# A fused attention and MoE kernel: one query load on another queue, seven more dummy matmuls near the start

## The chip, the cores and the metric

The kernel runs on one core of a Trainium2 chip. A core has five engines with their own instruction streams: TensorE (matrix products), VectorE, ScalarE, GpSimd (elementwise work) and SyncE (which here only issues transfers). ScalarE issues transfers too, on a queue of its own. The metric is device time in microseconds, the median over several runs.

## The reference

```python
q_s = exp(q - max(q, -1));  q_s /= sum(q_s, -1)      # softmax over the head's 64 columns
k_s = exp(k - max(k, 2));   k_s /= sum(k_s, 2)       # softmax over the 576 tokens
kv  = einsum('bhsd,bhse->bhde', k_s, v)              # 64 x 64 per batch and head
att = einsum('bhsd,bhde->bhse', q_s, kv)
x   = att.transpose(0, 2, 1, 3).reshape(4608, 512)
h   = x @ w_in                                       # 512 -> 2048
out = (h * sigmoid(beta * h)) @ w_out                # 2048 -> 512
```

There are 8 batches, 8 heads, 576 tokens and 64 columns per head, all float32.

## The kernel before, in words

**Slabs.** The 4608 tokens are cut into nine slabs: slab t (0 to 7) has the first 512 tokens of batch t, slab 8 the 64 that are left of each batch. For each slab there is a first pass (x times w_in, 16 groups f of 128 hidden columns, four matmuls m each, then SiLU on ScalarE into GT) and a second pass (GT times w_out into the output). Beside them, on ticks counted by matmuls, run the attention pieces of the next batches.

**Attention.** Heads go in pairs hp (0 to 3), 128 rows of the array together. For a pair: exp of Q and K on ScalarE (`exp_q`, `exp_kc`), cast of V (`cast_v`), normalisation of Q (`norm_main`: a reduction and a reciprocal on VectorE, a multiplication on VectorE or GpSimd), a turn of Q by four matmuls against the identity (`t_steps`) and a copy, the key-value product (18 small matmuls, `kv_tiles` or `kv_prods`), its scaling, and the output product with the turned Q (`out_now` or `out_prods`), whose result is copied into XT, the input of the first pass. From batch 2 on the turn is made by a DMA.

**The start.** Batch 0 has nothing to hide behind, so its pieces are written out by hand (lines 598 to 634). `warm(3, 0, True)` puts three long fp32 matmuls on zeros in front; `warm(n, bk)` puts n short bf16 ones (128x512, on the zeros of WARM) into bank bk. None of their results is used. Batch 0's order on TensorE is: long dummies, turn of pair 0, turns of beta (`turn_beta`), turn of pair 1, key-value product of pair 0, then by turns dummies, turns, key-value and output products of the later pairs, then the first matmuls of the first pass.

**Queues.** The order of loads is the order of `add` calls for each issuing engine. Line 291 loads batch 0's Q: pairs 0 and 2 whole on SyncE's queue, the four heads of pairs 1 and 3 (2, 3, 6, 7) one by one on ScalarE's, then beta (BT) there. SyncE goes on with K and V of batch 0 pair by pair, then w_in in twelve pieces, then w_out and batch 1. Every operation names what it reads and writes; `plan` turns this into waits on counters, and each engine works its own list in order.

**Batch 1** is worked during the second pass of slab 0 by the list `todo`: turns at ticks 104 and 109, key-value products in two halves at ticks 115 and 127. Its V pairs 1 to 3 are cast by GpSimd.

Of the kernel before, what the change touches and what calls it, by code (L numbers as in the profile page):

```python
# [29 lines left out]
PE, ACTE, DVE, POOL, SP = "tensor", "scalar", "vector", "gpsimd", "sync"  # L30
# [13 lines left out]
class Program:  # L44
# [12 lines left out]
    def add(self, eng, fn, r=(), w=(), bank=(), slot=None, after=()):  # L57
        op = Op(eng, fn, slot)
        op.pos = len(self.ops)
        deps = op.deps  # L60
        deps.extend(after)
        for k in r:
            deps.extend(self.writer.get(k, ()))
            self.readers.setdefault(k, []).append(op)
        for k in w:
            for d in self.readers.get(k, ()):
                if d is not op and not self._same(d, op):
                    deps.append(d)
            for d in self.writer.get(k, ()):
                if not self._same(d, op):  # L70
                    deps.append(d)
            self.readers[k] = []
            self.writer[k] = [op]
        for k in bank:
            t = self.touch.setdefault(k, {})
            for e, d in t.items():
                if e != eng:
                    deps.append(d)
            t[eng] = op
        if eng == POOL and slot is None:  # L80
            if self.pool is not None:
                deps.append(self.pool)
            self.pool = op
        self.ops.append(op)
        return op
# [78 lines left out]
def bass_efficient_attn_shen__then__act_swish_beta_kernel(  # L164
# [9 lines left out]
    qt_h, kt_h, vt_h = q.tensor, k.tensor, v.tensor  # L174
    win_h, wout_h, beta_h, out_h = moe_w_in.tensor, moe_w_out.tensor, moe_beta.tensor, out.tensor

    with ExitStack() as es:
        def sb(name, shape, dt):
            return es.enter_context(nc.sbuf_tensor(name, shape, dt))
# [4 lines left out]
        QF = [sb(f"QF{i}", [128, H, 4, D], F32) for i in range(2)]  # L184
# [38 lines left out]
        add = P.add  # L223
# [14 lines left out]
        def src(th, b, h0, nh):  # L238
            return bass.AP(th, (b * H + h0) * S * D, [[4 * D, 128], [S * D, nh], [1, 4 * D]])

        def dst(t, h0, nh):
            return bass.AP(t, h0 * 4 * D, [[H * 4 * D, 128], [4 * D, nh], [1, 4 * D]])
# [46 lines left out]


        for hp in range(NHP):
            eng = ACTE if hp % 2 else SP
            if hp % 2 == 0:
                add(eng, lambda e, hp=hp: e.dma_start(dst(QF[0], 2 * hp, 2), src(qt_h, 0, 2 * hp, 2)),
                    w=[("qf", 0, hp, hp // 2)], slot=f"qf0{hp}")
                continue
            for c in range(2):
                h = 2 * hp + c
                add(eng, lambda e, hp=hp, c=c, h=h: e.dma_start(  # L299
                    dst(QF[0], 2 * hp + 1 - c, 1), src(qt_h, 0, h, 1)),  # L300
                    w=[("qf", 0, hp, 2 + c)], slot=f"qf0{h}")
        add(ACTE, lambda e: e.dma_start(BT[:, :], bass.AP(beta_h, 0, [[512, 4], [1, 512]])),
# [29 lines left out]
        def norm_main(b, hp0, n, eng=DVE):  # L332
            i = b % 2
            a = bass.AP(EQ[i], hp0 * 512, [[2048, 128], [64, 8 * n], [1, 64]])
            s_ = bass.AP(QS[i], hp0 * 8, [[32, 128], [1, 8 * n]])
            v_ = bass.AP(QI[i], hp0 * 8, [[32, 128], [1, 8 * n]])
            vb = bass.AP(QI[i], hp0 * 8, [[32, 128], [1, 8 * n], [0, 64]])
            ks = [("eq", i, hp) for hp in range(hp0, hp0 + n)]
            add(DVE, lambda e: e.tensor_reduce(s_, a, AX.X, ALU.add), r=ks, w=[("qs", i, hp0)])  # L339
            add(DVE, lambda e: e.reciprocal(v_, s_), r=[("qs", i, hp0)], w=[("qi", i, hp0)])  # L340
            add(eng, lambda e: e.tensor_tensor(a, a, vb, ALU.mult), r=ks + [("qi", i, hp0)],  # L341
                w=ks)
# [22 lines left out]
        def bank(pool=MB):  # L365
            rot[0] += 1
            return pool[rot[0] % len(pool)]

        def mm(o, l, r_, start, stop, r=(), w=(), bk=0, tr=False, tp=None):
            if tr:  # L370
                add(PE, lambda e: e.transpose(o, l, r_), r=r, w=w, bank=[bk])  # L371
            else:
                add(PE, lambda e: e.matmul(o, l, r_, start=start, stop=stop, tile_position=tp),  # L373
                    r=r, w=w, bank=[bk])

        def t_steps(b, hps, pool=MB, eng=DVE):
            i = b % 2
            st = {}

            def one(n, hp, j):  # L380
                if n == 0 and j == 0:
                    st["b"] = bank(pool)
                p = PS[st["b"]]
                pb = p[:, :].bitcast(BF16)
                c = n * 512 + j * 128
                mm(pb[:, c:c + 128], bass.AP(EQ[i], hp * 512 + j * 128, [[2048, 128], [1, 128]]),
                   IDB[:, :], True, True, r=[("eq", i, hp), "idb"], w=[("ps", st["b"])],
                   bk=st["b"], tr=True)
                if n == len(hps) - 1 and j == 3:
                    w = len(hps) * 512  # L390
                    o = bass.AP(QT[i], hps[0] * 512, [[2048, 128], [1, w]])
                    add(eng, lambda e: (e.copy if eng == ACTE else e.tensor_copy)(o, pb[:, 0:w]),
                        r=[("ps", st["b"])], w=[("qt", i, h) for h in hps], bank=[st["b"]])
            return [lambda n=n, hp=hp, j=j: one(n, hp, j) for n, hp in enumerate(hps)
                    for j in range(4)]
# [110 lines left out]
        def warm(n, bk, long=False):  # L506
            for _ in range(n):
                if long:
                    mm(PS[bk][:, :], bass.AP(XT8, 0, [[NM * SM, 128], [1, 256]]).bitcast(F32),
                       bass.AP(XT8, 0, [[NM * SM, 128], [1, 1024]]).bitcast(F32), True, True,  # L510
                       r=["xw"], w=[("ps", bk)], bk=bk)
                else:
                    mm(PS[bk][:, :], WARM[:, 0:128], WARM[:, :], True, True, r=["warm"],
                       w=[("ps", bk)], bk=bk)
# [17 lines left out]
        def out_now(b, hp, bk, eng):  # L532
            i = b % 2
            for c in (0, 64):
                p = slice(c, c + 64)
                tile_mm(bk, c, 64 - c if hp % 2 else c, 0, SM, KVC[2][p, hp, :], QT[0][p, hp, :], True, True,
                        [("kvc", 2, hp), ("qt", 0, hp)])
            add(eng, lambda e: (e.copy if eng == ACTE else e.tensor_copy)(
                XT[i][:, hp, :], PS[bk][:, :]),
                r=[("ps", bk)], w=[("xt", i, hp)], bank=[bk])  # L540

        def go(steps):
            for s in steps:
                s()
# [28 lines left out]
        def cast_win(c, m, eng):  # L573
            add(eng, lambda e: e.tensor_copy(WIN[:, m, 512 * c:512 * c + 512], STAGE[c][:, m, :]),
                r=[SKEY[c][m]], w=[("win", c, m)])
# [3 lines left out]
        def turn_beta():  # L579
            for g, n, o in ((4, 4, 0), (2, 2, 0), (2, 2, 256)):  # L580
                for k_ in range(n):
                    mm(bass.AP(PS[KB], 16 + o // 128 + k_, [[512, 128], [4, g]]),
                       bass.AP(BT, o + k_, [[512, g], [n, 128]]), IDF[0:g, 0:g],
                       True, True, r=["bt", "idf"], w=[("ps", KB)], bk=KB, tr=True)
# [23 lines left out]
                cast_v(0, hp, ACTE)  # L608
        norm_main(0, 0, 1)
        norm_main(0, 1, 1, POOL)  # L610
        go(t_steps(0, (0,), (3,)))
        turn_beta()
        norm_main(0, 2, 1, POOL)
        norm_main(0, 3, 1, POOL)
# [14 lines left out]
        kv_tiles(2, 7)  # L629
        out_now(0, 1, 5, ACTE)  # L630
        cast_win(0, 0, DVE)
        warm(1, 3)
        out_now(0, 2, 0, ACTE)
        kv_tiles(3, 1)

# [1 line left out]

        def pass1_mm(t, f, m, bk):
            x = XT8 if t == 8 else XT[t % 2]
            rd = [("xt8", 0)] + [("xt8", p_, y) for p_ in range(1, 4) for y in range(2)] if t == 8 else [("xt", t % 2, m)]  # L640
            n = 2 if f < 8 else 4
            l = bass.AP(WIN, m * DFF + 128 * (f // n * n) + f % n, [[NM * DFF, 128], [n, 128]])
            mm(PS[bk][:, :], l, x[:, m, :], m == 0, m == NM - 1,
               r=rd + [("win", f // 4, m)], w=[("ps", bk)], bk=bk)
            if m == NM - 1:
                add(ACTE, lambda e: e.activation(GT[:, f, :], PS[bk][:, :], ACT.Silu,  # L646
                                                 scale=BETA[:, f:f + 1]),
                    r=[("ps", bk), "beta"], w=[("gt", f)], bank=[bk])
# [244 lines left out]
```

## Time and profile before

| what | value |
|---|---|
| median of 4 runs | 281.03 us (280.86 to 281.48) |
| profiled execution: time, span | 281.66 us, 279.8 us |
| TensorE busy | 270.8 us, 97% of the span |
| ScalarE, VectorE, GpSimd busy | 166.4, 102.9, 33.1 us |
| mean granted TensorE clock | 0.988 |
| HBM read, written | 36.71 MB, 9.44 MB |
| first matmul, first matmul of the first pass | 1.45 us, 16.03 us |

The span is from the first to the last instruction; the time has in addition what lies around it, 1.86 us in this execution. Matmul records carry modelled ends, so a busy TensorE may still run at half its clock; the granted clock is a column of its own. In a timeline row stand the start, the busy time, the engine, the line, what is written from what, and in brackets the idle time before it with its releaser. All matmuls are issued on line 373, all turns on line 371, so they are told apart by tiles.

### The profile page before, as it was taken

How to read it: one execution, taken by the hardware profiler on the slowest of the kernel's cores; microseconds unless marked ns; L12 is line 12 of the kernel's file. 1: busy time of each engine (PE TensorE's matmuls, PEld its weight loads, DVE VectorE, ACT ScalarE, POOL GpSimd, SP SyncE). 2: the span in 40 equal slices, each digit the busy share in tenths (PEclk: the TensorE clock that was granted, in tenths of full speed). 3: DMA queues.
4: the chain of work that ended last, by engine and by line, in shares of the span. 5: the costliest groups of instructions: out<-in, count | busy, mean ns of one | idle time of the engine just before them, and what ended most of it. 6: DMA issues, size and time to landing. Idle time of an engine off the chain costs nothing.

```text
span 279.8 us, 4581 instructions
## 1 busy us (share of the span) xinstructions
PE 270.8 (97%) x1892; PEld 131.8 (47%) x1922; DVE 102.9 (37%) x206; ACT 166.4 (59%) x240; POOL 33.1 (12%) x50
## 2 busy tenths in 40 slices
PE   6899999999999999999999999999999999999995
PEld 2545454454445454545454544444444444444443
DVE  3664595007590158305640463035603300110012
ACT  4657867789767835794479537853751276017500
POOL 2630041306100305030002100000000000000000
PEclk9689999999999999999999999999999999999999
DMA  7999999996279999960499134001600120011022
GB/s 224 389 387 402 388 389 374 375 380 113 41 238 389 200 356 290 374 147 2 144 357 234 39 130 95 2 4 75 169 0 2 47 103 2 0 73 77 2 71 79
DMA packets 42173, 50.12 MB, mean 179 GB/s; under 512 B 21028, under 2 KB 29476, under 8 KB 41000
## 3 DMA queue, kind: packets, MB, share of 16 engines
q1 hardware_dynamic: 41168, 48.77, 53.9%
q10 hardware_dynamic: 984, 1.06, 1.2%
q8 instruction: 15, 0.25, 0.4%
q14 instruction: 6, 0.05, 0.1%
HBM read 36.71 MB, written 9.44 MB: 165 GB/s over the span
## 4 chain that ended last, share of the span: by engine, by line
PE 94%; DMA 2%; issue 1%; ACTq 0%; ACT 0%; DVE 0%
PE PS L373 93%; DMA QF<-in_q_dram 2%; PE PS L371 1%; ACTq L299 0%; ACT EK L323 0%; ACT VB L358 0%; DVE O2S L722 0%; ACT EQ L315 0%; ACTq L147 0%
## 5 line engine op out<-in xcount | busy, mean ns | idle before, releaser
L646 ACT ACTIVATE GT<-PS,BETA 128x512 bf16<-128x512 f32 x144 | 96.7, 689 | 61.4 <-PE PS L373 61.4
L373 PE MATMUL PS<-WOUT,GT 128*128 128x512 bf16 (+2 forms) x573 | 125.0, 373 | 1.8 <-issue 1.3
L373 PE MATMUL PS<-XT,WIN 128*128 128x512 bf16 x566 | 125.7, 379 | 0.7 <-issue 0.2
L373 PEld LDWEIGHTS PS<-XT,WIN 128*128 128x128 bf16 x576 | 60.4, 106 | 63.6 <-ACT GT L646 0.4
L373 PEld LDWEIGHTS PS<-WOUT,GT 128*128 128x128 bf16 x592 | 56.5, 98 | 65.9 <-issue 1.1
L701 DVE COPY O2S<-PS 128x512 f32<-128x512 f32 x33 | 22.7, 688 | 124.3 <-PE PS L373 124.3
L358 POOL CAST VB<-VF 128x576 bf16<-128x576 f32 x29 | 20.8, 716 | 85.2 <-DMA VF<-in_v_dram 83.8
L339 DVE TENSOR_REDUCE QS<-EQ 128x8 f32<-128x512 bf16 (+1 forms) x22 | 20.1, 912 | 20.1 <-ACT EQ L315 20.0
L460 ACT CAST XT<-PS 128x512 bf16<-128x512 f32 x14 | 7.6, 588 | 23.9 <-PE PS L373 23.9
L323 ACT ACTIVATE EK<-KF 128x1152 bf16<-128x1152 f32 (+1 forms) x19 | 18.4, 1004 | 1.7 <-DMA KF<-in_k_dram 1.7
L315 ACT ACTIVATE EQ<-QF 128x512 bf16<-128x512 f32 x32 | 17.6, 615 | 3.0 <-DMA QF<-in_q_dram 3.0
L341 DVE TENSOR_TENSOR EQ<-EQ,QI 128x1024 bf16<-128x1024 bf16 (+1 forms) x14 | 16.2, 1158 | 0.5
L460 DVE CAST XT<-PS 128x512 bf16<-128x512 f32 x14 | 9.1, 686 | 13.4 <-PE PS L373 13.4
L341 POOL TENSOR_TENSOR EQ<-EQ,QI 128x512 bf16<-128x512 bf16 x8 | 8.3, 1042 | 34.9 <-DVE QI L340 34.5
L373 PEld LDWEIGHTS PS<-VB,EK 64*64 64x64 bf16 x576 | 7.3, 112 | 5.2 <-issue 2.5
L373 PE MATMUL PS<-VB,EK 64*64 64x65 bf16 x576 | 8.7, 199 | 0.9 <-ACT VB L358 0.5
L373 PE MATMUL PS<-QT,KVC 64*64 64x512 bf16 x64 | 6.8, 404 | 0.0
L646 ACT ACT_TABLE_LOAD x5 | 6.4, 1283 | 0.1
L373 PE MATMUL PS<-XT 128*128 128x512 f32 x6 | 4.9, 982 | 1.4 <-DVE XT L226 1.4
L340 DVE RECIPROCAL QI<-QS 128x8 f32<-128x8 f32 (+1 forms) x22 | 5.0, 226 | 0.8
L323 ACT ACT_TABLE_LOAD x4 | 5.1, 1283 | 0.1
L444 DVE TENSOR_TENSOR KVC<-PS,RC 128x128 bf16<-128x128 f32 (+1 forms) x16 | 4.4, 274 | 0.6
(51 smaller groups left out, 66.9 us busy)
## 6 DMA issues: line engine op xcount, KB each, us to landing
out_dram<-O2S SPq DMA_DIRECT2D x8, 1024.0 KB, 4.3
QF<-in_q_dram SPq DMA_DIRECT2D x30, 256.0 KB, 5.7
KF<-in_k_dram SPq DMA_DIRECT2D x6, 1152.0 KB, 8.1
VF<-in_v_dram SPq DMA_DIRECT2D x6, 1152.0 KB, 11.3
KF<-in_k_dram SPq DMA_DIRECT2D x8, 288.0 KB, 8.5
VF<-in_v_dram SPq DMA_DIRECT2D x8, 288.0 KB, 9.1
WST<-in_moe_w_in_dram SPq DMA_DIRECT2D x8, 256.0 KB, 7.6
O2S<-in_moe_w_in_dram SPq DMA_DIRECT2D x4, 512.0 KB, 11.0
```

The costliest lines, as they stand in the source:

```text
L315: add(ACTE, lambda e, o=o, a=a: e.activation(o, a, ACT.Exp), r=[("qf", i, hp, x) for x in ((2, 3) if hp % 2 else (hp // 2,))], w=[("eq", i ...
L323: add(ACTE, lambda e: e.activation(o, a, ACT.Exp), r=[("kf", i, h) for h in range(hp, hp + n)], w=[("ekc", i, h) for h in range(hp, hp + n)])
L339: add(DVE, lambda e: e.tensor_reduce(s_, a, AX.X, ALU.add), r=ks, w=[("qs", i, hp0)])
L340: add(DVE, lambda e: e.reciprocal(v_, s_), r=[("qs", i, hp0)], w=[("qi", i, hp0)])
L341: add(eng, lambda e: e.tensor_tensor(a, a, vb, ALU.mult), r=ks + [("qi", i, hp0)], w=ks)
L358: add(eng, lambda e: (e.copy if eng == ACTE else e.tensor_copy)(o, a), r=[("vf", i, hp), ("vone", i)], w=[("vb", i, hp, h) for h in ((0, 1 ...
L371: add(PE, lambda e: e.transpose(o, l, r_), r=r, w=w, bank=[bk])
L373: add(PE, lambda e: e.matmul(o, l, r_, start=start, stop=stop, tile_position=tp), r=r, w=w, bank=[bk])
L444: add(DVE, lambda e, o=o, p_=p_, vb=vb: e.tensor_tensor(o, p_, vb, ALU.mult), r=[("ps", bk)] + [("rc", i, hp) for hp in hps], w=[("kvc", k ...
L460: add(eng, lambda e, eng=eng, bk=bk, hp=hp: (e.copy if eng == ACTE else e.tensor_copy)(XT[i][:, hp, :], PS[bk][:, :]), r=[("ps", bk)], w=[ ...
L646: add(ACTE, lambda e: e.activation(GT[:, f, :], PS[bk][:, :], ACT.Silu, scale=BETA[:, f:f + 1]), r=[("ps", bk), "beta"], w=[("gt", f)], ba ...
L701: add(eng, lambda e: (e.copy if eng == ACTE else e.tensor_copy)(O2S[t % 2][:, u, :], PS[bk][:, :]), r=[("ps", bk)], w=[("o2", t % 2, u)], ...
```

## The change

Four edits. In the load loop, head 7 is issued by SyncE and no longer by ScalarE. Three short dummies are put in front of the turn of pair 0 and three behind it, in front of beta's turns. In front of the output product of pair 2 (the third) stand two short dummies in place of one. The list of what slab 8's first pass reads now names both halves of each of the four remainder pieces, where it named for the first piece a key that nothing writes.

```diff
         for hp in range(NHP):
-            eng = ACTE if hp % 2 else SP
             if hp % 2 == 0:
-                add(eng, lambda e, hp=hp: e.dma_start(dst(QF[0], 2 * hp, 2), src(qt_h, 0, 2 * hp, 2)),
+                add(SP, lambda e, hp=hp: e.dma_start(dst(QF[0], 2 * hp, 2), src(qt_h, 0, 2 * hp, 2)),
                     w=[("qf", 0, hp, hp // 2)], slot=f"qf0{hp}")
                 continue
             for c in range(2):
                 h = 2 * hp + c
-                add(eng, lambda e, hp=hp, c=c, h=h: e.dma_start(
+                add(SP if h == 7 else ACTE, lambda e, hp=hp, c=c, h=h: e.dma_start(
                     dst(QF[0], 2 * hp + 1 - c, 1), src(qt_h, 0, h, 1)),
                     w=[("qf", 0, hp, 2 + c)], slot=f"qf0{h}")
...
         norm_main(0, 1, 1, POOL)
+        warm(3, 0)
         go(t_steps(0, (0,), (3,)))
+        warm(3, 0)
         turn_beta()
...
         cast_win(0, 0, DVE)
-        warm(1, 3)
+        warm(2, 3)
         out_now(0, 2, 0, ACTE)
         kv_tiles(3, 1)
...
-            rd = [("xt8", 0)] + [("xt8", p_, y) for p_ in range(1, 4) for y in range(2)] if t == 8 else [("xt", t % 2, m)]
+            rd = ([("xt8", p_, y) for p_ in range(4) for y in range(2)] if t == 8
+                  else [("xt", t % 2, m)])
```

## The prediction

> **What bounds it now.** I began with the page: the chain of waits names TensorE for nearly everything, and the slices show its clock dipping only in the second and third slice (6 and 8 tenths). So the time is set by when TensorE gets into its dense stretch and by what interrupts it. Next I cut the start into stretches of 3.41 us, moving their edges until the granted clock was constant inside each:
>
> ```profile
> PE 94%; DMA 2%; issue 1%; ACTq 0%; ACT 0%; DVE 0%
> ```
> ```profile
> core 0: us, PE busy (x), PEclk, DMA share, GB/s
> 5.63:9.04 3.41, 2.21 (x14) 1.00 0.98 357
> 9.04:12.45 3.41, 2.85 (x36) 0.50 1.02 388
> 12.45:15.86 3.41, 3.05 (x61) 0.50 1.05 393
> 15.86:19.27 3.41, 3.36 (x28) 1.00 1.07 396
> ```
>
> The third figure from the right is the clock: full until 9.04, half until 15.86, then full to the end. Two equal steps of 3.41 us say that a monitor looks at fixed windows. The chain in order of time then shows what TensorE sat on before 10.20, and the timeline the waits:
>
> ```profile
> 2.17 6.14 DMA QF<-in_q_dram
> ...
> 8.39 0.07 ACT EQ L315
> 8.46 0.47 issue
> 8.92 0.67 ACT EK L323
> 9.59 0.57 ACT VB L358
> 10.16 0.04 issue
> 10.20 1.25 PE PS L373 x19
> ```
> ```profile
> 7.87 1.11 PE L371 MATMUL PS<-IDF,BT 4*128 4x4 f32 x8 [0.38 <-DMA BT<-in_moe_beta_dram]
> ...
> 8.39 0.63 ACT L315 ACTIVATE EQ<-QF 128x512 bf16<-128x512 f32 x1 [2.07 <-DMA QF<-in_q_dram]
> ...
> 11.51 0.66 POOL L358 CAST VB<-VF 128x576 bf16<-128x576 f32 x1 [0.28 <-DMA VF<-in_v_dram]
> ...
> 12.99 0.67 POOL L358 CAST VB<-VF 128x576 bf16<-128x576 f32 x1 [0.81 <-DMA VF<-in_v_dram]
> ...
> 14.34 2.85 POOL L574 CAST WIN<-WST 128x512 bf16<-128x512 f32 x4 [0.68 <-DMA WST<-in_moe_w_in_dram]
> ...
> 44.31 0.67 POOL L358 CAST VB<-VF 128x576 bf16<-128x576 f32 x1 [0.86 <-DMA VF<-in_v_dram]
> ...
> 45.84 0.48 PE L373 MATMUL PS<-VB,EK 64*64 64x65 bf16 x36
> ```
>
> In brackets stands the idle time and what ended it. Two things hold the start: ScalarE stands 2.07 us for head 7 (issued at 2.17, landed 8.31), and TensorE crawls at half clock from 9.04 to 15.86 with no gap left in it. The last two rows matter for the end: batch 1's fourth head pair is cast at 44.98 (44.31 + 0.67) and used at 45.84.
>
> **The queue.** Head 7 leaves ScalarE's queue (four issues of 0.47) for SyncE's, third there. Landings before, as issue plus time to landing: SyncE's heads 0,1 at 3.9 and heads 4,5 at 5.1; ScalarE's head 6 at 7.2, head 7 at 8.3; K pair 0 at 7.6, V pair 0 at 8.5, K and V pair 1 at 9.2 and 9.9, K pair 2 10.7. [...] Head 7 stands behind 5.1 with 128 KB against an equal partner: both it and head 6 land at about 6.0 (between 5.5 and, if head 6 doesn't profit, 7.2), so exp of pair 3 starts at 6.4 behind its predecessor (ends 6.32) and not at 8.39.
>
> What it is moved ahead of: twelve K, V loads and then all weight loads on SyncE's queue, issued 0.47 us later. The DMA share is 1.0 in nearly every microsecond from 6 to 50 and K, V land 6 to 7 us after issue, so they wait for bytes, not for the issue. By K pair 0 there are 83 KB more ahead of it: 0.23 us later, 7.8. From V pair 0 on the bytes ahead are the same: no shift (bounds: 0.3 earlier, since the dip at 5 to 6 us with share 0.71 could fill; 0.47 later, if the issue counted). Beta's load, now behind three heads and not four, lands before 7.87.
>
> ScalarE then: exp Q3 to 6.95, wait, exp K0 7.85 to 8.5, cast V0 to 9.15, exp K1 9.25 to 9.9, cast V1 to 10.6, exp K2 to 11.4, exp K3 12.2 to 12.9 (lands 12.21). The first key-value product may start at 9.2 instead of 10.20, **1.0 us**.
>
> **The dummies.** A 512-column bf16 matmul streams 0.216 us at full clock (steady spacing in the trace: 0.2157), 0.43 at half. Three start as the fp32 ones end (four passes at 0.85 each issue, last stream ends 5.9) and are through by 6.6, the first turn is ready at 7.1 (VectorE's normalisation): covered. Three more run 7.35 to 8.0; beta's turns follow, 1.1 us, to 9.1, against 8.98 now; the second turn waits for GpSimd until 9.05. Cost 0.1, and it dies in the wait to 9.2. The seventh costs 0.216 at full clock ahead of the third output product, where TensorE waits for V pair 3 until 13.7: nothing. Without this cover: 0.43 at half clock.
>
> What they buy is the clock. Columns streamed in 5.63:9.04 before: fp32 tail 0.27 us, four turns 0.21: about 14% of the window. With six dummies (1.28 us): 51%. The next windows at full clock hold 54 to 71% and 86%. At half clock, 9.04:12.45 held 68 to 86% (the products pair up or not) and was not enough to reopen; the next, full, was. So closing lies somewhere above 14%; no row shows 51%. [...] Gain if the gate stays open: half of the streaming; loss if it doesn't: bounded below. I take open, since 51% is a true filling and no longer an idle window.
>
> **The start, summed** at full clock: first product 9.2 to 9.6; second turn ready at 10.1 (GpSimd 9.03 + 1.04); second product after cast V1, 10.65; third turn after GpSimd's third pass, 11.25; third product after GpSimd's cast of V2, 12.2; output, two dummies, output to 13.45; fourth product after cast V3 (13.66) 13.7 to 14.05; first weight tile landed 13.6, cast by VectorE about 14.1; its four matmuls to 15.0; last output product; second row of weights at **15.25 against 17.33: 2.1 us**. GpSimd's casts of row 1, 2, 3 end at 15.05, 15.76, 16.5, needed 15.25, 16.1, 17.0: they fit.
>
> **What is late next.** From 17.33 TensorE is continuous. Moved by 2.1 us it meets loads whose landing is set by bytes: the last w_in cast ends 25.12 and is needed at 26.1, fits. Batch 1's first turn, now 38.93: w_out rows 8 to 11 land at 33.6 (VectorE scales them 35.09 now), then reduce 0.7, reciprocal 0.2, GpSimd 1.08, so 37.4: gain left 1.5. Second turn, two more reductions and a multiply behind: 39.05 against 40.43, left 1.4. Then the two rows shown last: V pair 3 of batch 1 lands at 44.2 and no byte before it is saved, so its product can't start before 45.05. It starts now at 45.84. **Left: 0.79 us.** After it, nothing in the list of TensorE's waits depends on a load; the later stages shift as one.
>
> The sum is against the profiled execution: 279.8 span, 281.66 with what lies around it, so 279.0 and 280.87. The median of the runs is 281.03, 0.63 lower; I move it by the same 0.79: **280.2 us**. The changed wait list of the last slab adds no instruction: slab 8's first product reads data that VectorE wrote long before.
>
> **Rivals.** *Gate falls at 9.04 all the same* and reopens at 15.86: the dense half-clock run starts at 9.66 (second turn ends) and not 10.20, and has one more dummy of 0.43: 0.11 gained, 280.9. For it: the unknown threshold. Against: a run packed from 9.05 may reopen at 12.45, which gives the forecast again.
>
> *Slower: the gate falls one window later*, at 12.45, because 9.04:12.45 with its waits for V1, GpSimd and V2 holds as little as 54%, and stays shut until 19.27. Then by 19.27 the dense part has run 0.32 + 1.7 us of full-speed work, where now it has 3.0: 1.0 lost, no load covers it, **282.0**. It decides if closing lies above 54 to 71%. Against: at half clock the work from 12.45 is packed, which reopened the gate at 15.86 before; then 0.68 is gained.
>
> *More*: the dip at 5 to 6 us fills or the queue change otherwise advances V by 0.3 to 0.6: the gain is then 1.1 to 1.4, 279.8.
>
> *The DMA shift is real*, 0.47 later everywhere: 0.79 - 0.47 = 0.3, 280.7; I count it to the forecast's lower part.
>
> **Numbers.** Forecast 0.55 (0.04 of it too small to see), gate falls early 0.22, slower 0.15, more 0.08. What can be told from no change is 0.2%, 0.56 us. Faster 0.51 + 0.08 = 0.59; slower 0.15 + 0.03 of the early fall with a dummy in the way; the rest, 0.23, within. Range 279.8 to 281.3: the clipped gain with its bounds, the early fall, and part of the slower case.
>
> **What would show it.** Clock 1.00 in 9.04:12.45 and 12.45:15.86; exp of Q pair 3 before 7; weights' second row near 15.3; the second turn's GpSimd release unmoved at 9.05; a wait of TensorE for GpSimd's VB cast at about 45. If that wait is missing with a gain under 0.8, the start fell short; if the clock is 0.50 after 12.45 in dense matmuls, I am wrong in sign.

## The result, and the profile after

| | before | changed |
|---|---|---|
| median | 281.11 us (63 runs) | 280.55 us (44 runs) |
| ratio, 95% interval | | 0.9982 (0.9975 to 0.9990) |
| profiled execution: time, span | 281.66, 279.8 us | 281.19, 279.4 us |
| second row of slab 0's weights starts | 17.34 us | 15.34 us |

The changed kernel is faster by 0.56 us, or 0.2%; 280.2 us was forecast, 0.91 us below the median of the kernel before in this table. The ratio came back in two later comparisons of the same pair: 0.9982 (0.9972 to 0.9992) and 0.9975 (0.9965 to 0.9986).

The granted clock of the changed kernel, by stretches of 3.41 us, follows; the third figure from the right is the clock. "Gate" is a name for whatever halves it: closed is a clock of 0.50 in that column, open one of 1.00. In the kept trace of this execution the first clock record, of 1.00, starts at 4.92 us (the last section has the weight loads on both sides of it), so the stretches are laid from about there.

```profile
core 0: us, PE busy (x), PEclk, DMA share, GB/s
4.97:8.38 3.41, 3.41 (x20) 1.00 0.98 335
8.38:11.79 3.41, 2.81 (x55) 1.00 1.05 399
11.79:15.20 3.41, 2.81 (x47) 1.00 1.02 379
```

In this execution the gate no longer closes: 1.00 in all three stretches. Next is the page's chain of work that ended last, which was TensorE for 94% before:

```profile
PE 82%; DMA 11%; SPq 4%; issue 1%; DVE 1%; POOL 0%
```

TensorE came so early that loads are now on the path. TensorE's timeline shows where they hold it, with what ended each wait in brackets:

```profile
36.93 0.39 PE L370 MATMUL PS<-IDB,EQ 128*128 128x128 bf16 x4
37.64 0.40 PE L370 MATMUL PS<-IDB,EQ 128*128 128x128 bf16 x4 [0.32 <-POOL EQ L340]
37.88 1.24 PE L372 MATMUL PS<-WOUT,GT 128*128 128x512 bf16 x5
39.31 0.62 PE L370 MATMUL PS<-IDB,EQ 128*128 128x128 bf16 x8 [0.19 <-DVE EQ L340]
39.77 1.46 PE L372 MATMUL PS<-WOUT,GT 128*128 128x512 bf16 x6
...
44.71 0.22 PE L372 MATMUL PS<-VB,EK 64*64 64x65 bf16 x2
45.45 0.48 PE L372 MATMUL PS<-VB,EK 64*64 64x65 bf16 x34 [0.52 <-POOL VB L357]
46.08 1.24 PE L372 MATMUL PS<-XT,WIN 128*128 128x512 bf16 x5 [0.16 <-issue]
```

The kernel before, at the same places:

```profile
38.93 0.61 PE L371 MATMUL PS<-IDB,EQ 128*128 128x128 bf16 x8
39.59 1.03 PE L373 MATMUL PS<-WOUT,GT 128*128 128x512 bf16 x4
40.90 1.46 PE L373 MATMUL PS<-WOUT,GT 128*128 128x512 bf16 x6
46.48 1.46 PE L373 MATMUL PS<-XT,WIN 128*128 128x512 bf16 x6 [0.16 <-issue]
```

Behind its first turn stand four matmuls but five weight loads, so the record of one matmul is missing there. The weight loads are complete in both profiles, before and changed:

```profile
39.32 0.80 PEld L373 LDWEIGHTS PS<-WOUT,GT 128*128 128x128 bf16 x5
37.82 0.80 PEld L372 LDWEIGHTS PS<-WOUT,GT 128*128 128x128 bf16 x5
```

Now follow one place after the other. The second row of weights is 2.0 us early. The weight loads behind batch 1's first turn are 1.5 us early (37.82 for 39.32). The matmuls behind the second turn are 1.1 us early (39.77 for 40.90), the first matmuls of slab 1 0.4 us (46.08 for 46.48). From there to the end both take 233.3 us (279.4 - 46.08, 279.8 - 46.48). So 1.6 of the 2.0 us is lost at three places between 36 and 46 us, all in waits for batch 1: its two turns and its last V pair. This is one execution of each kernel, and neither was a typical one: the profiled one of the changed kernel took 0.64 us more than its median. A table further on has the others.

The load that the change moves came earlier: exp of Q pair 3 starts at 7.10, not 8.39, though it still waits for its load:

```profile
7.10 0.63 ACT L314 ACTIVATE EQ<-QF 128x512 bf16<-128x512 f32 x1 [1.27 <-DMA QF<-in_q_dram]
```

### The profile page after: what moved, and what is told of

It reads as the page before. It is cut to its first block, busy times and chain, and to the rows that moved or that the text cites. A ratio compares the mean times of both kernels' runs of the same rounds, so it can differ in the third digit from the quotient of the medians.

```text
span 279.4 us, 4595 instructions
## 1 busy us (share of the span) xinstructions
PE 270.3 (97%) x1899; PEld 131.2 (47%) x1929; DVE 102.6 (37%) x206; ACT 166.5 (60%) x240; POOL 33.2 (12%) x50
## 4 chain that ended last, share of the span: by engine, by line
PE 82%; DMA 11%; SPq 4%; issue 1%; DVE 1%; POOL 0%
PE PS L372 82%; DMA VF<-in_v_dram 4%; DMA WST<-in_moe_w_out_dram 4%; DMA WST<-in_moe_w_in_dram 3%; SPq L250 2%; SPq L569 1%; DVE WOUT L562 1%; SPq L293 0%; POOL VB L357 0%; SPq L298 0%; DVE WIN L573 0%; DVE O2S L724 0%; SPq L558 0%; SPq L147 0%
## 5 line engine op out<-in xcount | busy, mean ns | idle before, releaser
L372 PE MATMUL PS<-VB,EK 64*64 64x65 bf16 x576 | 8.1, 193 | 1.5 <-POOL VB L357 0.9
L372 PEld LDWEIGHTS PS<-VB,EK 64*64 64x64 bf16 x576 | 6.6, 107 | 5.8 <-issue 2.5
L372 PE MATMUL PS<-QT,KVC 64*64 64x512 bf16 x64 | 6.2, 383 | 0.1
```

## The experiments

Each ratio is to the kernel before on the same chip, and each run has one profile.

**The kernel before, again.** No edit.

> The kernel before, unchanged. Gate theory with windows tied to the kernel's start: the clock falls at 9.0 and returns at 15.9 again, the mean clock of every run is near 0.988, and the ratio is 1.000 within 0.1%. Gate theory with free-running windows: the clock falls at some other moment, the mean clock differs between runs (0.988 for two half-rate windows, 0.994 for one, 1.000 for none), and runs with a higher clock are shorter, by up to 0.8 us.

280.98 us, ratio 0.9995 (0.9984 to 1.0006). The clock by windows in its profile:

```profile
7.69:11.10 3.41, 2.67 (x39) 1.00 1.04 407
11.10:14.51 3.41, 3.05 (x56) 0.50 1.05 391
14.51:17.92 3.41, 3.36 (x34) 1.00 1.05 387
```

The gate closed at 11.10 and for one window of 3.41 us (to 14.51), where the first profile had 9.04 and two (6.82 us, to 15.86). So the windows are not tied to the kernel's start. The steps of 3.41 us stand in the traces; that a monitor looks at fixed windows is the author's reading of them. A window at half rate takes 0.5 x 3.41 / 280 = 0.006 off the mean clock of a run, so every run's mean clock tells how many it had. All runs of the two kernels for which the clock was listed (before: 210 runs, these 14 and those of three comparisons; changed: 88 runs of three comparisons) sort like this:

| windows at half rate (mean clock) | before: runs, median | changed: runs, median |
|---|---|---|
| two (0.990 and below) | 78, 281.62 us | none |
| one (0.991 to 0.997) | 122, 280.88 us | 1, 280.77 us |
| none (0.998 and above) | 10, 280.76 us | 87, 280.49 us |

The change empties both upper rows. A run of before with two windows takes 1.1 us more than one of the changed kernel, one with one window 0.4 us. The free-running theory holds. That runs with a higher clock are shorter is clear between two windows and one (0.74 us), but not between one and none: 0.12 us, with ten runs in the last row and a standard deviation within each row of 0.3 to 0.4 us. These ten runs stand 0.27 us above the changed kernel, too few to call it a difference. So at least 0.74 of the 1.1 us in the first row is the windows' cost; how much of the 0.4 us in the second is, and how much another part of the change, stays open.

**Each half of the change alone.** The edits from here on are shown against the changed kernel. The load without the dummies:

```diff
-        warm(3, 0)
         go(t_steps(0, (0,), (3,)))
-        warm(3, 0)
...
-        warm(2, 3)
+        warm(1, 3)
```

> Head 7 on SyncE's queue, no added dummies. Gate theory: exp of Q pair 3 near 7.1 as in the changed kernel, but the clock falls near 9. If it stays low for two windows the gain over before is about 0.1 us (280.9 to 281.1); if the packed work from 9.05 reopens it after one window, the gain is that of the whole change, 0.5 us. Queue theory (the earlier exp is what counts): the whole gain, 0.5 us, with the clock low in 9 to 16.

280.69 us, ratio 0.9984 (0.9973 to 0.9995). In its profile the clock falls at 8.39 us, 3.41 us behind 4.98, where the changed kernel's first clock record starts at 4.92, so by chance the windows lie in nearly the same place:

```profile
4.97:8.38 3.41, 2.49 (x15) 1.00 1.04 373
8.38:11.79 3.41, 3.23 (x48) 0.50 1.04 384
11.79:15.20 3.41, 3.09 (x55) 1.00 1.01 354
```

Without the dummies the first of these windows has gaps (2.49 us busy), and the gate closes behind it; with them it has none (3.41) and the gate stays open. Both figures have modelled ends, so they are not the share of time in which columns streamed. The two kernels differ in the dummies alone, and the windows in 0.06 us, so this pair shows what the dummies do. Here the gate opens again after one window, which held 3.23 us of work. Over its 22 runs, 7 had no half-rate window, 12 one, 3 two; in the 65 runs of before beside them it was 4, 39 and 22. So the load alone brings most of the gain, and in part by shifting runs into better rows of the table, which the queue theory did not have. Within each row it also stands 0.2 to 0.3 us below before on this chip (280.39 for 280.69, 280.77 for 281.01, 281.23 for 281.56), but with 7, 12 and 3 runs that is a hint only.

The dummies without the load, run twice:

```diff
-                add(SP if h == 7 else ACTE, ...
+                add(ACTE, ...
```

> All seven dummies, head 7 still on ScalarE's queue. Gate theory: exp of Q pair 3 at 8.4 as before, first key-value product at 10.2, clock 1.0 throughout, second row of weights near 15.4, and the whole gain of 0.5 us, since what clips it comes later. Queue theory: no gain, ratio to before 1.000.

> The seven dummies without the moved load, beside the changed kernel on the same chip. If the moved load is worth something with the gate open (the earlier comparison hints at 0.2 us), this is 0.1 to 0.3 us above the changed kernel; if the gate is all, it is equal within 0.1 us.

280.80 us, ratio 0.9987 (0.9977 to 0.9997), and 280.55 us, 0.9984 (0.9973 to 0.9994), where the changed kernel beside the second had 280.51 us:

> The changed kernel again, as the base for the other three on the same chip: 0.5 to 0.7 us below before, mean clock 0.998 or more in every run.

The changed kernel's ratio here was 0.9975 (0.9965 to 0.9986), with 21 runs without a half-rate window and 1 with one. With dummies alone 38 of 42 runs had none, and 4 had one. So with the gate open the moved load is worth nothing that these runs can tell (0.04 us on the same chip). The profiles agree: without it the second row of weights starts at 14.89 and 15.17 us, no later than with it (15.34). Each half alone gives most of the gain, and together they leave 1 of 88 runs with a window at half rate.

**How many dummies.** Three (behind the turn only), six without the seventh, and twelve:

```diff
-        warm(3, 0)
         go(t_steps(0, (0,), (3,)))
         warm(3, 0)
```
```diff
-        warm(2, 3)
+        warm(1, 3)
```
```diff
-        warm(3, 0)
+        warm(6, 0)
         go(t_steps(0, (0,), (3,)))
-        warm(3, 0)
+        warm(6, 0)
```

> The changed kernel without the three dummies in front of the first turn (three behind it and the seventh stay). Gate theory: windows over the start now hold about a third of streaming; if closing needs less than a third, the mean clock stays at 1.000 in all runs and the time is the changed kernel's; if more, some runs show 0.994 or 0.988 and are up to 0.5 us longer.

> The changed kernel without the seventh dummy. If the seventh holds the gate open in the window of the third output product, some of the runs show a mean clock of 0.994 or less; if it does nothing, all show 0.998 or more and the time is the changed kernel's within 0.1 us.

> Six dummies in front of the first turn and six behind it, in place of three and three: 1.3 us more of streaming. Clip theory: the first turn starts near 7.2, the second near 9.4, the first key-value product 0.6 to 0.8 us later than in the changed kernel, and the waits for batch 0's later V pairs and at batch 1's turns take this up, so the time rises by 0 to 0.2 us. Rival (the start passes straight to the end): it rises by 0.6 to 0.8 us.

Three: 280.60 us, ratio 0.9983 (0.9972 to 0.9994), 21 of 22 runs without a half-rate window. Six without the seventh: 280.60, 0.9983 (0.9971 to 0.9994), 13 of 14. Twelve: 280.46, 0.9977 (0.9966 to 0.9987), 21 of 21. Three of the six would nearly do, the seventh shows nothing, and the longer start of the twelve costs nothing in the time. From none (the load alone) to three, the runs with a lost window fall from 15 of 22 to 1 of 22; what more dummies add beyond that, 1 in 22 against 0 in 21, can't be told. In the profile with twelve the first key-value product started at 10.98 us, in the changed kernel's of the third comparison at 9.89. The first pair of rows shows batch 1's first turn with twelve, the second pair that of the changed kernel:

```profile
37.69 0.61 PE L370 MATMUL PS<-IDB,EQ 128*128 128x128 bf16 x8
38.13 0.59 PE L372 MATMUL PS<-WOUT,GT 128*128 128x512 bf16 x2
```
```profile
36.88 0.39 PE L370 MATMUL PS<-IDB,EQ 128*128 128x128 bf16 x4
37.77 0.40 PE L370 MATMUL PS<-IDB,EQ 128*128 128x128 bf16 x4 [0.51 <-POOL EQ L340]
38.00 0.81 PE L372 MATMUL PS<-WOUT,GT 128*128 128x512 bf16 x3
```

The changed kernel comes 0.8 us earlier and waits; behind the turn the two are 0.13 us apart. So a start that is 0.8 us late is paid back here.

**What takes the gain back.** The changed kernel as base:

> The changed kernel, unchanged, as the base for the other three on the same chip: ratio to before 0.998, mean clock 0.998 or more in every run.

280.43 us, ratio 0.9982 (0.9972 to 0.9992), all 22 runs with the full clock. On the same chip, without the loads of w_out rows 14 and 15 (their products use the old contents of the staging buffer):

```diff
-        load_wout(14, 1)
-        load_wout(15, 1)
```

> The changed kernel without the loads of w_out rows 14 and 15 of each sixteen (512 KB; those products use what the staging buffer still holds). Clip theory, bytes: K and V pairs 2 and 3 of batch 1 land 1.2 to 1.4 us earlier (V pair 3 near 42.5 to 43.3), TensorE's wait for its cast goes, and the time falls by 0.1 to 0.5 us below the changed kernel; the waits at batch 1's two turns, before those loads, stay. Rival (the landing is set by the moment of issue): the V pair lands within 0.3 us of where it did.

280.49 us, ratio 0.9973 (0.9962 to 0.9983). The cast of batch 1's last V pair stands at

```profile
42.58 0.67 POOL L357 CAST VB<-VF 128x576 bf16<-128x576 f32 x1 [0.89 <-DMA VF<-in_v_dram]
```

and not at 43.6 to 44.7 as in the thirteen profiles that load all. So with 512 KB fewer ahead of it the cast starts at least 1.0 us earlier: here the bytes ahead set the landing, and TensorE's wait for it is gone. But the median is that of the base, so this landing is not what holds the median run. The two turns before it are what is left. The chain of the changed kernel in the third comparison runs through the second turn (start, length, what):

```profile
22.90 11.16 DMA O2S<-in_moe_w_out_dram
34.06 0.03 issue
34.09 1.67 DVE WOUT L562 x4
35.76 0.60 DVE QS L338
...
38.20 1.19 DVE EQ L340
39.39 0.05 issue
39.44 0.62 PE PS L370 x8
```

w_out rows 8 to 11 land at 34.06; VectorE scales them, does three reductions and a multiplication, and TensorE turns. No work of TensorE stands in this chain before the turn.

The profiles of the two kernels side by side, in us, show how much one execution differs from the next, and what stays fixed:

| profile | time | second row of slab 0 | VectorE begins on w_out rows 8 to 11 | product with the V pair begins | V pair's cast ends | first matmul of slab 1 |
|---|---|---|---|---|---|---|
| before, first (two windows) | 281.66 | 17.34 | 35.09 | 45.84 | 44.98 | 46.48 |
| before, again (one window) | 280.66 | 16.08 | 34.11 | 44.86 | 44.87 | 45.56 |
| changed, first | 281.19 | 15.34 | 33.96 | 44.71 | 45.40 | 46.08 |
| changed, second | 280.64 | 16.21 | 34.09 | 44.84 | 44.84 | 45.52 |
| changed, third | 280.71 | 15.19 | 34.09 | 44.84 | 44.90 | 45.59 |

From the last column to the end of the span all five take 233.2 to 233.4 us, so what differs between executions lies before it. The product begins 10.75 us behind VectorE's scaling in every row, whatever the start was. That holds in the profile with fewer bytes too, and within 0.01 us in those of the other runs above. So VectorE's chain, with the turns at its end, sets the product. It can't begin before its load: the rows in the first profile of before and in the third of the changed kernel are

```profile
35.09 1.67 DVE L563 TENSOR_SCALAR WOUT<-O2S,RB 128x512 bf16<-128x512 f32 x4
34.09 1.67 DVE L562 TENSOR_SCALAR WOUT<-O2S,RB 128x512 bf16<-128x512 f32 x4 [0.86 <-DMA O2S<-in_moe_w_out_dram]
```

Only after the start with two half-rate windows is VectorE itself late, by about 1 us, and has no wait for the load. In the one profile with one window nothing of that loss is left here. On top comes the V pair. Without a wait the product takes 0.64 us to slab 1 (first row), so the V pair cost 0.73 us in the changed kernel's first profile, but 0.04 and 0.11 in the other two. No run moved the loads of w_out rows 8 to 11, so this last step is read from the profiles, not tested by an edit.

Two more runs give TensorE other work at the V pair. Both move the second half of batch 1's key-value product behind three matmuls of slab 1; the second opens slab 1 by rows over six groups instead of five, so that more stands behind each product. The second diff shows only what it has beyond the first:

```diff
-                        (127, lambda: kv_half(1, (7, 0), 2))]
...
                 at(0, 0, 3)
+                kv_half(1, (7, 0), 2)
                 at(1, 0, 3)
+                at(0, 3, 4)
+                at(1, 3, 4)
                 out_half(1, (7, 7, 7, 0), 2)
...
-                at(0, 3)
-                at(1, 3)
+                at(0, 4)
+                at(1, 4)
```
```diff
-        FIRST = (16, 5)
+        FIRST = (16, 6)
...
+                o2_evac(0, 3, 6, DVE)
                 at(0, 0, 3)
                 ...
-                o2_evac(0, 3, 6, DVE)
```

> The changed kernel, with the second half of batch 1's key-value product (pairs 2 and 3) moved behind the first three matmuls of slab 1 (and two more matmuls put in front of the output product that follows it). Clip theory (the landing of batch 1's last V pair takes back what the start gains): the wait of 0.52 us for GpSimd's cast near 45 goes, and the time falls by 0.3 to 0.6 us below the changed kernel, to 280.0 to 280.2. Rival (the gain is lost at other places before it): the wait goes and another takes its place, time as the changed kernel within 0.1 us.

> The changed kernel with the late half of batch 1's key-value product behind three matmuls of slab 1, as in the run before, but with six groups of slab 1 by rows and not five, so that five matmuls follow that product and four the output product. Clip theory: TensorE no longer waits for GpSimd's cast near 45 and no other wait takes its place; 0.1 us in executions where the V pair lands early (43.8), 0.5 to 0.7 where it lands late, so the median falls by 0.1 to 0.4 us below the changed kernel and its upper tail shrinks. Rival (the clip is not what holds the median run): same as the changed kernel within 0.1 us.

280.71 us (ratio 0.9989, 0.9981 to 0.9997) and 281.09 us (1.0005, 0.9990 to 1.0019). The first shows the rival: the cast no longer holds TensorE there, and a wait of 0.24 us for VectorE's copy of XT stands behind the output product. The second was slower than the changed kernel beside it (280.43). TensorE's timeline shows what came in its place:

```profile
53.80 1.48 PE L372 MATMUL PS<-XT,WIN 128*128 128x512 bf16 x6 [0.58 <-ACT GT L648]
```

The groups behind the six wait for a SiLU on ScalarE (0.58 us here; one takes 689 ns on the changed kernel's page), and the changed kernel has no wait at this place. Why the SiLU comes too late with six groups and not with five is not shown by a run. No version here beats the changed kernel clearly.

## Why the prediction was right, and where it was off

**The dummies keep the gate open: right.** This is shown by the pair of profiles with windows in the same place and by 87 of 88 runs. The slower rival (the gate falls one window later and stays shut for two) was seen in no run of the changed kernel.

**The start: right in size, and close by luck.** 15.25 was forecast for the second row of weights and 15.34 measured; 9.2 for the first key-value product and 9.19. But the other two profiles of the changed kernel have 16.21 and 15.19 for the one, 9.99 and 9.89 for the other, so a hit within 0.1 us is luck. Inside it, exp of Q pair 3 started at 7.10, not 6.4, because head 7 came at 7.0 (issue 1.75 plus 5.3), not 6.0; K pair 0 covered for that, as in the sum. The other two profiles have 7.38 and 6.40 here. No run shows the 83 KB more that the sum puts ahead of K pair 0 and the 0.23 us that it takes for them: K pair 0 landed at about 7.66 (issue 2.26 plus 5.4), 0.1 us behind before (1.76 plus 5.8), and its exp started at 7.68, where the sum had 7.85.

Two terms inside were wrong. The sum counted the issue of head 7 as a cost to SyncE and nothing as saved on ScalarE. ScalarE did save it: its first exp starts 0.49 us earlier. The first turn came at 6.62 for 7.11 and the second at 8.63 for 9.05; with the load alone the first came at 6.62 too, with the dummies alone at 7.11 and 7.10. The exps before and changed:

```profile
4.67 1.65 ACT L315 ACTIVATE EQ<-QF 128x512 bf16<-128x512 f32 x3
4.18 1.65 ACT L314 ACTIVATE EQ<-QF 128x512 bf16<-128x512 f32 x3
```

So the sign "second turn unmoved at 9.05" failed. And the dummies in front of the first turn were priced at 0.1 us for a gate that opens by 5.63. In the third profile the fp32 dummies run at half rate to their end: the last two weight loads at 4.18 and 5.03 take 0.33 us each, and the next two, of short dummies, stand 0.86 us apart (5.88 and 6.74), for 0.43 in the first profile (5.41 and 5.84). There the first turn starts at 7.55, and the first product at 9.89 though its V was cast by 8.86. Neither error shows in the second row of weights. It comes at 15.19 in that third profile, and at 14.89 and 15.17 with the dummies alone, which have neither the saved issue nor the 1.0 us that the sum gives to the queue.

**The losses on the way: right in place.** The forecast left 1.5, 1.4 and 0.79 us after the two turns and the V pair; the profile has 1.5, 1.1 and 0.4. The V pair's cast started 0.42 us later in this execution than in the one of before (44.73 for 44.31). In the thirteen profiles that load all it starts between 43.6 and 44.7, so one profile could not give this term to better than half a microsecond. The forecast took the V pair as what decides. The run with fewer bytes shows that without it the median stays, so something else holds it as well: by the profiles VectorE's chain and its turns.

**The term that was mis-sized is the last one**, where 0.79 us from the profiled execution was moved onto the median. That execution had two half-rate windows, as 78 of 210 runs; the commonest run has one. From two windows the gain is 281.62 - 280.49 = 1.1 us, more than forecast, from one it is 0.4. The mixture over all, by the counts, is 0.37 x 1.13 + 0.58 x 0.39 + 0.05 x 0.27 = 0.66 us; the first comparison had 0.56. The profiled execution stood 0.63 us over the median of the runs, which was a hint that it wasn't the common one. That 0.79 came out so near to 0.56 is in part luck: it is the gain of a run with two windows, cut down by a V pair that cost next to nothing in the changed kernel's other two profiles.

**A reading that was wrong and cost nothing:** the clock "full until 9.04". The last section has it.

**The edit in slab 8's list** was priced at nothing. The stretch from slab 1 on, which holds it, has the same length in both profiles; no run has this edit alone.

## What to carry to other kernels

Where the granted clock falls at another moment in each execution, as here (9.04 and 11.10 us in two profiles of one kernel), one profile shows one draw. Take the mean clock of every run, sort the runs by it, and price the change by class, not from the trace at hand. Short dummies in the waits of this start were cheap insurance, since later waits absorbed their cost; the runs with three, six, seven and twelve were hardly told apart (280.43 to 280.60 us). Before valuing an earlier start, walk forward to the next transfers that are set by bytes: in the first two profiles 2.0 us at 15 us were 0.4 us at 46.

## What was not expected of the hardware

The column of the granted clock reads 1.00 from the start, but TensorE began at about half rate. The fp32 weight loads tell it, all of the same shape. The first pair of rows is the changed kernel, the second the kernel before (start, length):

```profile
4.17 0.34 PEld L372 LDWEIGHTS PS<-XT 128*128 128x128 f32 x1 [0.52 <-issue]
4.98 0.19 PEld L372 LDWEIGHTS PS<-XT 128*128 128x128 f32 x1 [0.47 <-issue]
```
```profile
4.17 0.34 PEld L373 LDWEIGHTS PS<-XT 128*128 128x128 f32 x1 [0.52 <-issue]
5.02 0.34 PEld L373 LDWEIGHTS PS<-XT 128*128 128x128 f32 x1 [0.52 <-issue]
```

0.34 us turns into 0.19 between 4.17 and 4.98 in one, whose first clock record starts at 4.92, and not yet at 5.02 in the other, whose first starts at 5.62. So in both the weight loads are slow before the first record, and the column shows nothing before it. In the kernel before, run again, full rate came later still: its first turn, at 7.11, took 0.58 us, where that of the first profile, at 7.11 too, took 0.38 and a later one in the second, at 9.31, 0.40. In the first profile the half clock comes 3.41 us behind the first record, at 9.04; in the second, 3.41 us ahead of the fall at 11.10 is 7.69, between the slow turn and the fast one. So in these two the moment of the full rate says which later window is the thin one. It does not explain all of the spread: the 87 runs of the changed kernel without a half-rate window still reach from 280.1 to 282.45 us.

No long gap was needed for the gate to close. The window 4.97 to 8.38 with the load alone had 2.49 us of modelled work in it and no wait of TensorE over 0.59 us, and behind it the clock was 0.50. Which filling between this one and that of the three dummies is enough stays open.
